# Loads of all 128 rows, paced loads at the start, n1 visits of three halves, and an n2 visit between transform and last stage

## The chip, the cores and the metric

One core of one Trainium2 chip. The metric is the device time of one execution in microseconds, median of several runs; lower is better.

## The reference

```python
# x: (8, 6336, 128), h: (6336, 128)
y = irfft(rfft(x, n=2*S, axis=1) * rfft(h, n=2*S, axis=0), n=2*S)[:, :S]   # causal convolution per channel
scores = y @ w_gate
for b in range(8):
    top = argpartition(-scores[b], 128)[:128]          # 128 rows of each batch
    xe = y[b, top]
    ye = maximum(xe @ w1, 0) @ w2                      # 128 -> 1024 -> 128
    out[b, top] = y[b, top] + sigmoid(scores[b, top])[:, None] * ye
```

## The kernel before

The convolution is done by transforms written as matmuls. 6336 = 99 x 64, so a transform over time is one over n1 (99 points) and one over n2 (64 points). A **unit** is two batches times 64 channels; there are eight (i = 0 to 7). The filter h is treated like one more unit, ahead of them. A unit comes in eight **blocks** of eight channels, each a load of 120 rows of 4 KB (`load_x`, g counts blocks: 0 to 7 are h, 8 to 15 unit 0, and so on). A row holds two halves, `fold` makes their difference (L154, into another buffer) and their sum (L156, in place), on VectorE or GpSimd.

Stages of a unit:

- **n1 transform**, `stage_a`: a block is two **halves** (q = 0, 1); a half is 16 matmuls (L167) into one of three PSUM buffers `pb` and a copy to SBUF by ScalarE (L176), or VectorE (L173).
- **n2 transform**, `stage_b`: 13 chunks of up to 8 of the 99 frequencies. A chunk is 32 matmuls (L204), four products with h's transform on VectorE (L213, which free the PSUM buffer) and two sums on GpSimd (L224). It then loads the table and the h piece three chunks ahead (`load_w` L190, `load_h` L196).
- **inverse n2**, `stage_c`: 16 **items** of 16 matmuls (L308), each ended by ScalarE's copy (L312). Between them, `weigh` sums the scores on VectorE (64 instructions a unit, L292).
- **inverse n1** or last stage, `stage_d`: 16 items (L338), every two of them copied (L349) and stored.

A traced matmul of 32-bit data is two passes, so a half shows as 32 matmuls on the profile's timeline, and an item as 32.

The eight units run as a software pipeline. In the loop of unit i there are 32 items: 0 to 15 are `stage_c` of unit i, 16 to 31 its `stage_d`. Into them a hand-written plan puts **visits** of unit i+1: n1 visits of one block (two halves) ahead of items 0, 1, 3, 4, 6, 7, 9 and 10, and n2 visits of two chunks ahead of items 12, 14, 17, 19, 22, 24 and 27 (the last of one chunk). Items 1 to 6 also issue the first tables and h pieces of unit i+1. Each engine and SP's DMA queue run their instructions in the order written. `load_x(g + 5)` follows a block's n1 visit and waits for it, since there are five load buffers (`RX`).

Scores, the choice of 128 rows (`pick`, a search by counting in eleven steps, each some VectorE work and one small matmul, L414), the gathers, the expert's matmuls (L530, L542) and the scatters run as coroutines. `aside()` lets them issue their next step when an estimate of TensorE's time (`t["pe"]`) has passed the time they gave. Units 2, 4 and 6 carry the end of a search in their first half, units 3, 5 and 7 two experts.

Ahead of the loop, 16 blocks (h and unit 0) are loaded, folded on VectorE and transformed, with five warm-up matmuls before them; then `stage_b_first` (L254) does n2 for h and unit 0 together. All 16 loads are issued at once, as far as SP's queue takes them:

```python
sp.dma_start(out=fa, in_=fa_d)
for g in range(16):
    load_x(g)
```

## Time and profile before

| | us |
|---|---|
| runs (median of 3) | 947.28 |
| runs, lowest and highest | 943.19, 947.48 |
| the profiled execution | 941.33 |
| its span, first to last instruction | 939.5 |

The page gives, for one execution, each engine's busy time, TensorE's granted clock (PEclk, in tenths of full speed), the DMA queues, and groups of instructions by source line. The other views answer for a stretch of time: busy time by stretch, waits with what ended them ("issue" means that the profile shows nothing that the engine waited for), the timeline, and the chain of work that ended last. In `out<-in` the names are the program's tiles: `xr` a loaded block, `slots` the large buffer of transforms, `two` fold results, `pb` a PSUM buffer, `tx` products, `ht` h pieces, `at` and `tab_wb` tables.

### The profile page before, as it was taken

Reading aid. Unit: us, or ns where it says so; the run is one execution under the profiler, and the core shown is the slowest. Engines: PE = TensorE matmul, PEld = TensorE weight load, DVE = VectorE, ACT = ScalarE, POOL = GpSimd, SP = SyncE. Lnnn points to the kernel's source line nnn. Section 1 sums busy time; section 2 is a strip of 40 time slices with the busy share of each in tenths; the row PEclk is TensorE's granted clock in tenths of the full one; section 3 lists DMA queues with packets and bytes.
Section 4 is the critical chain, followed back from the end, with each engine's and each line's share of the span. In section 5 each row is a group of like instructions: output and inputs, shape, how many; then the busy total and the mean of one; then the engine's idle time right before and its main releaser. Section 6 shows DMA issues by size and latency. Waiting matters only on the chain.

```text
span 939.5 us, 37070 instructions
## 1 busy us (share of the span) xinstructions
PE 882.4 (94%) x16558; PEld 777.0 (83%) x16558; DVE 674.3 (72%) x1571; ACT 348.5 (37%) x405; POOL 344.3 (37%) x292
## 2 busy tenths in 40 slices
PE   7789899999998989999999899998999999999996
PEld 5689898889886878878987798887987798879875
DVE  5558966757596996756479897756559898687571
ACT  3533562147211741145411462135511373115321
POOL 0048426612463026620546027640346204460103
PEclk8699999999999999999999999999999999999999
DMA  8759767767574846765566665747457464751051
GB/s 215 195 182 331 219 173 227 246 167 203 169 247 162 235 116 195 240 184 145 139 191 203 177 171 178 260 151 182 109 155 262 147 175 121 238 171 52 16 178 42
DMA packets 66513, 168.38 MB, mean 179 GB/s; under 512 B 9713, under 2 KB 26063, under 8 KB 66354
## 3 DMA queue, kind: packets, MB, share of 16 engines
q1 hardware_dynamic: 65330, 164.96, 59.2%
q8 instruction: 130, 2.13, 1.0%
q0 software_dynamic: 1024, 1.05, 0.4%
q14 instruction: 29, 0.24, 0.1%
HBM read 133.02 MB, written 32.96 MB: 177 GB/s over the span
## 4 chain that ended last, share of the span: by engine, by line
PE 74%; DVE 16%; issue 5%; ACT 2%; DMA 2%; POOL 1%; POOLq 0%; ACTq 0%; DVEq 0%
PE pb L338 21%; PE pb L308 21%; PE pb L204 14%; PE pb L167 10%; DVE acc L292 5%; PE pb L254 4%; DVE tx L213 2%; DVE slots L213 2%; DVE cmp L405 2%; PE m L530 1%; ACT slots L312 1%; PE m L542 1%; DVE xr L156 1%; DMA slots<-tab_wb 1%; DVE num L408 1%
## 5 line engine op out<-in xcount | busy, mean ns | idle before, releaser
L224 POOL TENSOR_TENSOR slots<-slots,tx 128x512 f32<-128x512 f32 (+1 forms) x182 | 231.5, 1304 | 213.6 <-DVE tx L213 200.0
L308 PE MATMUL pb<-wc,slots 64*99 64x128 f32 x4096 | 254.0, 276 | 6.9 <-DVE tx L213 5.1
L308 PEld LDWEIGHTS pb<-wc,slots 64*99 64x99 f32 x4096 | 232.5, 169 | 19.5 <-issue 4.7
L338 PE MATMUL pb<-slots,at 99*99 99x256 f32 (+1 forms) x1040 | 234.3, 376 | 11.1 <-ACT slots L312 9.8
L338 PEld LDWEIGHTS pb<-slots,at 99*99 99x99 f32 x1040 | 159.7, 163 | 63.1 <-ACT slots L312 11.5
L312 ACT COPY slots<-pb 99x1024 f32<-99x1024 f32 x128 | 143.4, 1121 | 177.2 <-PE pb L308 156.8
L204 PEld LDWEIGHTS pb<-slots 128*64 128x64 f32 x5544 | 169.8, 137 | 19.9 <-issue 16.0
L204 PE MATMUL pb<-slots 128*64 128x64 f32 x5544 | 177.5, 222 | 5.9 <-DVE tx L213 3.4
L292 DVE SCALAR_TENSOR_TENSOR acc<-slots,wgl,acc 128x198 f32<-128x198 f32 x496 | 179.0, 436 | 0.9 <-POOL slots L224 0.9
L213 DVE TENSOR_TENSOR slots<-pb,ht 128x512 f32<-128x512 f32 (+1 forms) x182 | 120.0, 660 | 80.8 <-PE pb L204 59.0
L349 ACT COPY yt<-pb 99x1024 f32<-99x1024 f32 x63 | 63.9, 1015 | 306.6 <-PE pb L338 304.0
L176 ACT COPY slots<-pb 128x792 f32<-128x792 f32 x138 | 117.1, 904 | 40.9 <-PE pb L167 40.9
L213 DVE TENSOR_TENSOR tx<-pb,ht 128x512 f32<-128x512 f32 (+1 forms) x182 | 119.6, 657 | 0.0
L167 PE MATMUL pb<-fa,xr 50*64 50x99 f32 x1952 | 102.7, 255 | 9.0 <-issue 8.1
L167 PEld LDWEIGHTS pb<-fa,xr 50*64 50x64 f32 x1952 | 90.8, 138 | 17.7 <-issue 12.1
L154 POOL TENSOR_TENSOR two<-xr 120x512 f32<-120x512 f32 x12 | 25.5, 2129 | 143.1 <-PE pb L167 143.1
L167 PE MATMUL pb<-fa,two 50*64 50x99 f32 x1344 | 69.6, 253 | 0.0
L167 PE MATMUL pb<-fa,slots 50*64 50x99 f32 x1312 | 55.1, 278 | 13.4 <-issue 13.4
L546 POOL DMA_INDIRECT out<-xe,iu x16 | 16.2, 1012 | 132.5 <-DVE xe L544 129.5
L269 POOL TENSOR_TENSOR slots<-slots,tx 128x256 f32<-128x256 f32 (+1 forms) x50 | 39.4, 810 | 65.0 <-DVE tx L266 63.8
L167 PEld LDWEIGHTS pb<-fa,slots 50*64 50x64 f32 x1312 | 50.1, 156 | 15.9 <-issue 14.6
L167 PEld LDWEIGHTS pb<-fa,two 50*64 50x64 f32 x1344 | 61.0, 136 | 0.2 <-issue 0.2
(140 smaller groups left out, 613.7 us busy)
## 6 DMA issues: line engine op xcount, KB each, us to landing
slots<-tab_wb SPq DMA_DIRECT2D x86, 512.0 KB
xr<-in_x SPq DMA_DIRECT2D x61, 480.0 KB
out<-yt SPq DMA_DIRECT2D x63, 396.0 KB
ht<-hd SPq DMA_DIRECT2D x84, 256.0 KB
at<-tab_at SPq DMA_DIRECT2D x128, 153.1 KB
hd<-slots SPq DMA_DIRECT2D x12, 512.0 KB
xr<-tab_wb SPq DMA_DIRECT2D x9, 512.0 KB
slots<-in_h SPq DMA_DIRECT2D x8, 480.0 KB
```

Source lines behind the costliest of these rows:

```text
L167: pe.matmul(pt[c * 64:c * 64 + 64, b, d * N1:(d + 1) * N1], src, fa[rows, c], start=True, stop=True)
L176: act.copy(out=dst, in_=src)
L204: pe.matmul(banks[c][g * 64:g * 64 + 64, j * 64:j * 64 + 64], wt[:, j, c * 64:c * 64 + 64], y[:, g, :, k0 + j], start=True, stop=True)
L213: v.tensor_tensor(out=dst, in0=banks[c][:, 0:kn * 64].rearrange("p (k b j t) -> p k b j t", k=kn, b=2, t=2), in1=ht[t].rearrange("p k (j t ...
L224: pool.tensor_tensor(out=d3, in0=d3, in1=tx.rearrange("p k (j t) -> p k j t", t=2), op=ALU.add if c else ALU.subtract)
L254: pe.matmul(pair[g * 64:g * 64 + 64, c, j * 128:j * 128 + 128], wt[:, q + j, c * 64:c * 64 + 64], both[:, :, g, :, k0 + q + j], start=True ...
L269: pool.tensor_tensor(out=d3, in0=d3, in1=tx[:, c, 0:w].rearrange("p k (j t) -> p k j t", t=2), op=ALU.add if c else ALU.subtract)
L292: v.scalar_tensor_tensor(out=dst, in0=col, scalar=w, in1=dst, op0=ALU.mult, op1=ALU.add)
L308: pe.matmul(pair[0:N1, g, s % 4 * 128:s % 4 * 128 + 128], y[rows, s // 2, ri, :, s % 2], wc[rows, ri], start=(ri == 0), stop=(ri == 1))
L312: act.copy(out=z[:, s // 4], in_=pair[0:N1].rearrange("p g (j t m) -> p (g j) t m", j=2, t=2))
L338: pe.matmul(pt[0:N1, o:o + w * 128], ats[tau // 2][:, tau % 2, c], z[:, c, q:q + w], start=(c == 0), stop=(c == 1))
L349: act.copy(out=yt.rearrange("p n b q d -> p n q b d"), in_=src.rearrange("p (n q b d) -> p n q b d", n=w, q=4, b=2))
```

## The change

- A block's load and folds take all 128 rows instead of 120 (rows 114 to 127 hold zeros in DRAM already).
- At the start four loads are issued; each later one comes behind a fold. A memset of one element of its buffer on VectorE, right behind that fold, is what the load waits for. The memset `ones16` moves behind six folds; the warm-up is 48 matmuls of 64 columns instead of 5 of 512, on a smaller memset.
- n1 visits are of three halves ahead of items 0, 2, 4 and 6 and of four ahead of item 8. Folds and loads go along with their blocks.
- n2 visits at 14, 17, 19, 22, 24 become 14, 16, 19, 22, 25: the one at 16 stands between the last item of `stage_c` and the first of `stage_d`.
- The first tables and h pieces of the next unit are issued at items 1, 3, 5, 7, 9 and 10, not 1 to 6.
- In the last unit `aside()` is called in every step of the last stage, and twice ahead of item 16; the second expert of unit 7 is held before its output matmuls until item 16.

```diff
-    def load_x(g):
+    def load_x(g, paced=False):
...
-        sp.dma_start(out=raw[g][0:XR], in_=src[0:XR, n].rearrange("p (s d n) -> p s d n", s=2, d=8))
+        if paced:
+            v.memset(raw[g][0:1, 0, 0, 0:1], 0.0)
+        sp.dma_start(out=raw[g], in_=src[:, n].rearrange("p (s d n) -> p s d n", s=2, d=8))
...
-    def stage_a(g, r, dve=()):
-        a, o = raw.pop(g), odd.pop(g)
+    def stage_a(g, r, dve=(), halves=(0, 1)):
+        a, o = raw[g], odd[g]
         n = g % 8
-        for q in range(2):
+        for q in halves:
...
-                if w == 2 and tau != 2:
+                if (w == 2 and tau != 2) or i == NU - 1:
                     aside()
...
-                for _ in g:
+                for n, _ in enumerate(g):
                     yield after_act(1.7)
+                    while work is apart and g is todo[1] and n == 2 and place[0] < 16:
+                        yield 1
...
-        for g in range(16):
+        for g in range(4):
             load_x(g)
-        plain = acc.rearrange("p t b c k -> p (t b c k)")
+        plain = acc.rearrange("p t b c k -> p (t b c k)")[:, 0:128]
         v.memset(plain, 1.0)
-        for _ in range(5):
-            pe.matmul(psb()[:, 0], plain[:, 0:128], plain[:, 0:512], start=True, stop=True)
-        v.memset(ones16, 1.0)
+        for _ in range(3):
+            pt = psb()
+            for k in range(16):
+                pe.matmul(pt[:, k // 8, k % 8 * 64:k % 8 * 64 + 64], plain, plain[:, 0:64], start=True, stop=True)
         for g in range(6):
             fold(g, v)
+            load_x(g + 4, True)
+        v.memset(ones16, 1.0)
         for g in range(16):
             if g < 10:
                 fold(g + 6, v)
+                if g < 6:
+                    load_x(g + 10, True)
...
-                for n, at_item in enumerate((0, 1, 3, 4, 6, 7, 9, 10)):
-                    plan[at_item] = [("a", n)]
+                for n, at_item in enumerate((0, 0, 0, 2, 2, 2, 4, 4, 4, 6, 6, 6, 8, 8, 8, 8)):
+                    plan.setdefault(at_item, []).append(("a", n))
...
+                if i == NU - 1 and item == 16:
+                    ready[1] = 0.0
+                    aside()
+                    aside()
...
-                            g = g0 + k
-                            if g % 8 < 6:
+                            g, q = g0 + k // 2, k % 2
+                            if q == 0 and g % 8 < 6:
                                 fold(g + 2, v)
                                 on_dve(1.4)
-                            elif g % 8 == 7:
+                            elif q == 0 and g % 8 == 7:
                                 fold(g + 1, pool)
-                            stage_a(g, (i + 1) % 2)
-                            load_x(g + RX)
-                            if g % 8 == 7:
+                            stage_a(g, (i + 1) % 2, (), (q,))
+                            if q:
+                                load_x(g + RX)
+                            if q and g % 8 == 7:
                                 fold(g + 2, pool)
```

What moves, on the engines' own queues (line numbers of the changed kernel are one or more higher).

VectorE at the very start, before:

```order
L603 MEMSET acc 128x792
L606 MEMSET ones_84 128x128
L154 TENSOR_TENSOR slots<-slots 120x512
L156 TENSOR_TENSOR slots<-slots 120x512
L154 TENSOR_TENSOR slots<-slots 120x512
```

and in the changed kernel, where L139 is the memset that a load waits for:

```order
L606 MEMSET acc 128x128
L155 TENSOR_TENSOR slots<-slots 128x512
L157 TENSOR_TENSOR slots<-slots 128x512
L139 MEMSET slots 1x1
L155 TENSOR_TENSOR slots<-slots 128x512
L157 TENSOR_TENSOR slots<-slots 128x512
L139 MEMSET slots 1x1
```

The first memset is shorter, the second has gone behind the sixth fold, and each fold pair is followed by one tiny memset.

TensorE at the turn from `stage_c` (L308) to `stage_d` (L338) in the loop of unit 0, with the n2 visits (L204) of unit 1, before:

```order
L308 MATMUL pb<-wc,slots 99x128 x32
L204 MATMUL pb<-slots 64x64 x64
L308 MATMUL pb<-wc,slots 99x128 x32
L338 MATMUL pb<-slots,at 99x128 x4
L338 MATMUL pb<-slots,at 99x256 x2
L204 MATMUL pb<-slots 64x64 x64
L338 MATMUL pb<-slots,at 99x256 x8
```

and in the changed kernel (L309, L339 and L205 are the same lines):

```order
L309 MATMUL pb<-wc,slots 99x128 x32
L205 MATMUL pb<-slots 64x64 x64
L309 MATMUL pb<-wc,slots 99x128 x32
L205 MATMUL pb<-slots 64x64 x64
L339 MATMUL pb<-slots,at 99x128 x4
L339 MATMUL pb<-slots,at 99x256 x10
```

The visit has moved from behind the first item of the last stage to ahead of it.

ScalarE in the first half of unit 0, where L176 copies a half and L312 an item, before:

```order
L176 COPY slots<-pb 128x2x2x2x99 x2
L312 COPY slots<-pb 99x4x2x128
L176 COPY slots<-pb 128x2x2x2x99 x2
L312 COPY slots<-pb 99x4x2x128 x2
L176 COPY slots<-pb 128x2x2x2x99 x2
```

and in the changed kernel (L177 and L313):

```order
L177 COPY slots<-pb 128x2x2x2x99 x3
L313 COPY slots<-pb 99x4x2x128 x2
L177 COPY slots<-pb 128x2x2x2x99 x3
L313 COPY slots<-pb 99x4x2x128 x2
L177 COPY slots<-pb 128x2x2x2x99 x3
```

Two halves to one or two items have become three halves to two items.

## Rows read from the trace of the kernel before

**Rows 1.** The page: section 1 (busy time of each engine) and the instruction queue of section 3.

```profile
PE 882.4 (94%) x16558; PEld 777.0 (83%) x16558; DVE 674.3 (72%) x1571; ACT 348.5 (37%) x405; POOL 344.3 (37%) x292
...
q8 instruction: 130, 2.13, 1.0%
```

**Rows 2.** Busy time by stretch: stretch, length, busy (count) by engine, PEclk, DMA share, GB/s.

```profile
0.00:53.20 53.20, 38.80 (x1034) 33.08 (x1034) 27.95 (x39) 23.52 (x27) 0.20 (x4) 0.81 0.77 201
...
308.00:364.00 56.00, 50.87 (x1220) 47.93 (x1218) 51.29 (x122) 29.56 (x32) 15.38 (x12) 0.97 0.67 184
...
85.00:90.00 5.00, 5.00 (x92) 5.00 (x90) 4.14 (x13) 1.51 (x3) 3.90 (x6) 1.00 1.00 351
```

**Rows 3.** TensorE's waits in units 0 to 6: total us, times, longest.

```profile
PE pb L167 <- issue: 8.9, 5, 3.6
PE pb L338 <- ACT slots L312: 8.3, 7, 1.2
...
PE pb L338 <- DVE tx L213: 1.3, 3, 0.4
```

**Rows 4.** Timeline of TensorE in the start: start us, us, instructions, idle before.

```profile
18.49 5.55 PE L167 MATMUL pb<-fa,slots 50*64 50x99 f32 x127 [4.12 <-issue]
26.80 5.01 PE L167 MATMUL pb<-fa,slots 50*64 50x99 f32 x127 [2.76 <-issue]
34.83 2.09 PE L167 MATMUL pb<-fa,slots 50*64 50x99 f32 x44 [3.02 <-issue]
...
47.19 3.04 PE L167 MATMUL pb<-fa,slots 50*64 50x99 f32 x127 [0.80 <-issue]
51.90 1.41 PE L167 MATMUL pb<-fa,slots 50*64 50x99 f32 x51 [1.67 <-issue]
...
54.47 5.75 PE L254 MATMUL pb<-slots,xr 128*64 128x128 f32 x96 [0.80 <-DVE slots L173]
```

**Rows 5.** DMA queues from 5 to 35 us: packets, MB, share of 16 engines.

```profile
DMA packets 1918, 7.04 MB, mean 235 GB/s; under 512 B 208, under 2 KB 208, under 8 KB 1915
...
q1 hardware_dynamic: 1915, 6.99, 95.7%
q8 instruction: 3, 0.05, 0.8%
```

**Rows 6.** Timeline of VectorE in the start, the folds of blocks.

```profile
5.77 0.69 DVE L154 TENSOR_TENSOR slots<-slots 120x512 f32<-120x512 f32 x1 [3.93 <-DMA slots<-in_h]
6.50 0.69 DVE L156 TENSOR_TENSOR slots<-slots 120x512 f32<-120x512 f32 x1
7.91 0.69 DVE L154 TENSOR_TENSOR slots<-slots 120x512 f32<-120x512 f32 x1 [0.72 <-DMA slots<-in_h]
...
39.77 0.69 DVE L154 TENSOR_TENSOR slots<-slots 120x512 f32<-120x512 f32 x1 [1.22 <-PE pb L167]
```

**Rows 7.** Groups of instructions: count | busy us, mean ns | idle before.

```profile
L213 DVE TENSOR_TENSOR tx<-pb,ht 128x512 f32<-128x512 f32 (+1 forms) x182 | 119.6, 657 | 0.0
L176 ACT COPY slots<-pb 128x792 f32<-128x792 f32 x138 | 117.1, 904 | 40.9 <-PE pb L167 40.9
```

**Rows 8.** Timeline of TensorE in the units, at four waits.

```profile
154.25 1.99 PE L338 MATMUL pb<-slots,at 99*99 99x128 f32 x12 [1.18 <-ACT slots L312]
...
287.57 2.72 PE L204 MATMUL pb<-slots 128*64 128x64 f32 x46 [3.39 <-DVE tx L213]
...
351.99 3.63 PE L308 MATMUL pb<-wc,slots 64*99 64x128 f32 x32 [3.80 <-DVE tx L213]
...
888.24 2.00 PE L338 MATMUL pb<-slots,at 99*99 99x128 f32 x12 [1.54 <-ACT slots L312]
```

**Rows 9.** The chain that ended last: an n2 visit, an item, an n1 visit.

```profile
383.42 3.93 PE pb L204 x128
...
411.88 1.93 PE pb L308 x32
413.81 1.52 PE pb L167 x62
```

More of the change, by code (lines that the diff above doesn't have):

```diff
@@ L26 @@
 NT = 33
-XR = 120
 ZS = 128 * 128
@@ L143, in fold @@
             return
-        a = raw[g][0:XR]
+        a = raw[g]
         if g < 16:
@@ L151, in fold @@
         odd[g] = o.rearrange("p (d n) -> p d n", d=8)
-        o = odd[g][0:XR]
+        o = odd[g]
         if part < 2:
@@ L629, in conv_moe @@
             if i < NU - 1:
-                for n, at_item in enumerate((0, 1, 3, 4, 6, 7, 9, 10)):
-                    plan[at_item] = [("a", n)]
-                for n, at_item in enumerate((12, 14, 17, 19, 22, 24, 27)):
+                for n, at_item in enumerate((0, 0, 0, 2, 2, 2, 4, 4, 4, 6, 6, 6, 8, 8, 8, 8)):
+                    plan.setdefault(at_item, []).append(("a", n))
+                for n, at_item in enumerate((12, 14, 16, 19, 22, 25, 27)):
                     plan[at_item] = [("b", k) for k in range(2 * n, min(NC, 2 * n + 2))]
@@ L644, in conv_moe @@
                     load_constants(2)
-                if i < NU - 1 and 1 <= item < 7:
-                    (load_h if item % 2 == 0 else load_w)((i + 1) % 2, (item - 1) // 2)
+                if i < NU - 1 and item in (1, 3, 5, 7, 9, 10):
+                    k = (1, 3, 5, 7, 9, 10).index(item)
+                    (load_h if k % 2 else load_w)((i + 1) % 2, k // 2)
                 if 0 <= item - at_first < RA:
                     load_at(item - at_first)
+                if i == NU - 1 and item == 16:
+                    ready[1] = 0.0
+                    aside()
+                    aside()
                 if item in plan:
```

## The prediction

> **What bounds the kernel now.** I read the page first, then the busy times by stage, then the waits of TensorE, and last the timelines at the places that these named. TensorE is busy for 882.4 us, 94% of the span [rows 1], so the kernel is TensorE's queue with holes in it, and the question is which holes the change closes. The profiled execution took 941.33 us, 1.8 us more than its span; the three other runs took 943.19 to 947.48 us. The sum below is made on 941.33 and moved by +4 us at the end, about the middle between the profiled run and the median.
>
> The holes lie in three places. First the start: in the first 53.2 us TensorE is busy for 38.8 us at a mean clock of 0.81 [rows 2]. Second the eight units: between 104 and 845 us TensorE waits 8.9 us for nothing that the profile shows, always in front of the n1 transform, 8.3 us for ScalarE in front of the last stage, and 1.3 us there for product buffers [rows 3]. Third, units 2, 4 and 6 have a first half in which VectorE itself is nearly full: 51.29 of 56 us [rows 2].
>
> In the start, three pauses of 4.12, 2.76 and 3.02 us stand in front of runs of about 127 matmuls, with no releaser [rows 4]. The page counts 130 packets on the instruction queue, and matmuls and weight loads together 33,116: one packet for every 255 instructions, or 127 matmuls with their weight loads [rows 1]. So I read these pauses as TensorE waiting for its next packet of instructions while the loads fill the DMA engines: from 5 to 35 us only 3 such packets moved, with the engines 95.7% taken by the loads [rows 5]. The runs of 127 start 8.0 to 8.3 us apart there. At 47 to 52 us, where 512 KB loads run, they start 4.71 us apart [rows 4].
>
> **The change, part by part.**
>
> Loads of 128 rows. A block of 120 rows arrives every 2.13 us (the folds of h start at 5.77, 7.91 and so on, each waiting for its load) [rows 6], and the stretch with only such loads moves 235 GB/s [rows 5]. The kernel's 128-row traffic between 85 and 90 us, mostly 512 KB pieces, moves 351 GB/s [rows 2]. A block of 524,288 bytes would take 1.49 us at that rate, 2.23 us at the old one. I take 1.5 us, because the traffic at 85 to 90 us goes in the same 128 pieces of 4 KB as the new loads. The Trainium skill (DMA: Bandwidth & Descriptors, "Why a DMA increments its semaphore by 16 and not by 1") says that a transfer is spread over the largest count up to 16 that divides its outer dimension: 15 for 120 rows, 16 for 128. By that alone each engine moves eight rows either way, a block still takes 2.13 us and the start gives nothing, as in rival (2); the two rates in the rows differ by far more than 16 to 15, which only a run can explain.
>
> Four loads ahead. VectorE gets one tiny memset behind each of the first twelve folds, and each load from the fifth waits for its own memset. The trace has none so small; between 0 and 0.2 us each, I take 0.1 us. A fold pair holds VectorE for 1.4 us [rows 6], so it needs 1.5 us a block, as the loads do. The first block lands some 0.6 us sooner (2.13 less 1.5), so folding begins near 5.1 us, the sixteenth fold near 5.1 + 15 x 1.55 = 28.4 us and ends near 29.8 us; before, it began at 39.77 us [rows 6]. Behind the waiting loads on SP stand only the next loads and the first table loads, which wait for TensorE anyway. What is late next is ScalarE: the first ten blocks give it 20 copies of 904 ns [rows 7], about 18.4 us, from some 9.7 us on, to 28 us. Then six blocks at TensorE's 1.52 us [rows 9] and a copy on VectorE end near 38.5 us. That is the best case. The worst is 8.0 us a packet until the loads end: by 28.4 us only some seven blocks are through (two and a half from the packets that are there at the start, then two per 8 us from 18.5 us on), and the other nine, at 1.52 us and shorter pauses, end near 46 us. I take 42.5 us, by the 4.71 us spacing beside fast loads. The second stage begins at 54.47 us now [rows 4]: **-12 us**, ends -8 and -16. The warm-up of 48 narrow matmuls instead of 5 wide ones, the shorter memset ahead of it and the memset moved behind six folds have only VectorE's and TensorE's wait for the first load to fill, so 0.
>
> The visit between the stages. In units 0 to 6 the last stage begins with a wait of 1.18 us for ScalarE's last copy (154.25 is one of seven) [rows 8]. The change puts the n2 visit of 64 matmuls, 3.93 us long [rows 9], into that place, so the copy is covered. The visit needs a buffer that the one two items before has used; VectorE frees it 1.96 + 2 x 4 x 0.66 = 7.2 us after that visit began [rows 7], and TensorE comes back after 3.93 + 2 x 1.93 = 7.8 us [rows 9]. So it just fits. The visit's table and h loads are issued by the visits at items 12 and 14, at least 7 us ahead. 7 x 1.18 = 8.3; I take **-7 us** (0 to -8.3). In the last unit the second expert's 8 output matmuls go into the same gap, 1.54 us [rows 8]: **-1.5**.
>
> Three halves to a visit. TensorE's work is the same: two items and three halves are 2 x 1.93 + 3 x 0.76 = 6.1 us [rows 9]. A half's copy is 904 ns [rows 7], so three halves in a row leave ScalarE some 0.5 us behind, four 0.6 us, and the items behind them give that back before the three buffers come round. Eight blocks are through at item 8 instead of 10. The folds come earlier, so VectorE has no less to do before the first n2 visit: in unit 2 it frees that visit's buffers at 351.99 us after 45 us without a pause, and TensorE waits 3.80 us [rows 8]. That hole does not close: VectorE has the same work in front of it. Part of it moves to the visit at item 8, whose last fold now has 33 weighings ahead of it on VectorE instead of 38, while TensorE gets there 3.8 us sooner. **0** (0 to +3).
>
> Loads spread out. Until item 4 a unit now issues 4 x blocks, one table and one h load, where it issued 4, 2 and 2: 2.8 MB instead of 3.5, and the x part at 1.5 us instead of 2.13 us a block. The pauses without releaser in the units, five of 8.9 us in all and 3.6 us at most [rows 3], all stand in front of the n1 transform, where these loads run, and after a pause TensorE runs slower for a while: 32 passes took 3.63 us after the wait of 3.80 us [rows 8] against 1.93 elsewhere [rows 9], as at half the granted clock. Against it, item 8 issues 64 transform matmuls without an item between: 128 passes and as many weight loads in 3.04 us, where 4.2 us was the shortest for a packet. I take **-4 us** (+4 to -8.9).
>
> Small ones. The n2 visits of the last stage stand three items apart; that covers the 1.3 us for product buffers [rows 3] and gives the 3.39 us wait of unit 1 one item, 1.8 us, more room [rows 8]: **-3** (0 to -4.7).
>
> Sum: 12 + 7 + 1.5 + 4 + 3 = 27.5; 941.33 - 27.5 = 913.8 us as profiled, **918 us** for a median. All good ends together: 16 + 8.3 + 1.5 + 8.9 + 4.7 = 39.4, 906 us. All bad ends together: 8 + 1.5 - 4 - 3 = 2.5, 943 us.
>
> **Rivals.**
>
> (1) The refill stays slow: loads land faster, but a packet of instructions keeps taking 8 us while they run. For it: three packets in 30 us. Against: 4.71 us beside faster loads. The start gives 8 instead of 12 and the units nothing for their pauses: -19.5, **926 us**.
>
> (2) The 120 rows are not what makes those loads slow, since both x and h are read with 32 KB from row to row. Then a block takes 2.23 us, the last fold begins near 5.9 + 15 x 2.23 = 39.4 us as before, and the start gives nothing: -15.5, **930 us**. Against: no row of the trace separates pitch from row count. The Trainium skill has a rule here that speaks against the change (DMA: Bandwidth & Descriptors, "Latency and other measured facts": large power-of-two row pitches slow DMA copies; its figures begin at 512 KiB); no run here shows it yet.
>
> (3) The change does not cover the turn: a search step of VectorE slips between the products of the visits at items 14 and 16 and takes more than the 0.6 us to spare, so that a wait for VectorE of about the old size replaces the 1.18 us for ScalarE. The order shows the steps at items 12 and 16, so the price is the seven turns, +7 us: **925 us**.
>
> (4) Slower: the visit of four halves at item 8 outruns the instruction packets in every unit. A pause like the longest, 3.6 us [rows 3], with the slow passes after it costs 3.6 + 1.7 = 5.3 us; one in each of seven units is 37 us against the 27.5 gained, and it decides from 4 us per unit on: **955 us**. Against: five such waits in all seven units now, and the shortened interval is at one place in a unit.
>
> **How the numbers follow.** Forecast 0.63, (1) 0.18, (2) 0.08, (3) 0.07, (4) 0.04. The range 903 to 935 us holds the forecast with its good ends and the first three rivals; it leaves out (4) and the all-bad corner. A measurement of this kernel can tell about 0.5%, here below 942.5 or above 952.0 us. Only (4) and the corner are not faster: faster 0.93, same 0.04, slower 0.03.
>
> **What would show it.** Folds of the start 1.5 to 1.6 us apart and the second stage beginning at 39 to 46 us; no TensorE wait for ScalarE's copy at the turns; fewer than 5 us without releaser in the units; the wait of VectorE in units 2, 4 and 6 still there, some of it in front of the n1 transform. The prediction is wrong if folds stay 2.1 us apart, if the turn has a wait for VectorE, or if pauses in front of the n1 transform grow past 20 us.

## The result, and the profile after

| | us |
|---|---|
| before, median of 4 runs beside it | 945.24 |
| after, median of 4 runs (lowest, highest) | 918.71 (917.17, 921.89) |
| after / before, with 95% interval | 0.973 (0.968 to 0.979) |
| the profiled execution of after, its span | 921.89, 920.1 |

The forecast was 918 us. By the ratio the change gave 25 us (20 to 31) where the sum had 27.5. The two profiled executions, on which the readings below rest, differ by 19.4 us; that of after was the longest of its four, that of before shorter than three of the four runs beside it. The terms of the sum did not hold: in these profiles the start, which was to give 12 us, cost 4.5 us, and the units gave 24 us where 15.5 had been counted for them.

In the kernel after, lines stand one higher up to the loop (L168 is L167 of before, L309 is L308, L339 is L338, L214 is L213); the warm-up is L610. First the busy time by stretch (stretch, length, busy time and count by engine, PEclk, DMA share, GB/s), of before: the start, units 0, 1, 3 and 4.

```profile
0.00:100.08 100.08, 84.89 (x1826) 78.73 (x1827) 63.68 (x135) 37.73 (x51) 35.18 (x49) 0.90 0.77 231
100.08:200.26 100.18, 96.03 (x1949) 84.36 (x1948) 66.09 (x148) 38.39 (x41) 44.41 (x36) 1.00 0.69 205
200.26:306.27 106.01, 100.73 (x1975) 88.52 (x1974) 80.31 (x177) 38.89 (x40) 39.12 (x30) 0.98 0.68 197
...
410.29:526.08 115.79, 111.04 (x2041) 96.56 (x2040) 82.69 (x187) 42.04 (x52) 43.15 (x34) 0.99 0.59 172
526.08:629.43 103.35, 98.75 (x1964) 86.77 (x1964) 80.47 (x184) 38.75 (x40) 48.21 (x34) 0.98 0.66 192
```

The same stretches of after:

```profile
0.00:104.59 104.59, 96.82 (x1912) 94.62 (x1912) 62.51 (x147) 36.98 (x51) 35.17 (x49) 0.97 0.66 228
104.59:201.75 97.16, 95.15 (x1949) 84.29 (x1948) 66.30 (x148) 38.60 (x41) 47.20 (x36) 1.00 0.67 214
201.75:300.97 99.22, 97.39 (x1975) 86.43 (x1974) 81.11 (x177) 38.82 (x40) 42.92 (x30) 1.00 0.68 213
...
404.59:514.47 109.88, 108.58 (x2041) 95.25 (x2040) 83.89 (x187) 42.14 (x52) 43.88 (x34) 1.00 0.58 184
514.47:617.21 102.74, 97.29 (x1965) 86.62 (x1964) 82.87 (x183) 38.56 (x40) 42.36 (x34) 0.97 0.62 196
```

Read the lengths first: the start grew by 4.5 us; unit 0 lost 3.0 us, unit 1 6.8 us, unit 3 5.9 us, unit 4 only 0.6 us. Then TensorE's busy time for the same passes: in unit 3 it fell by 2.5 us, in unit 1 by 3.3 us. So in these two profiles a unit gains in two ways, by shorter waits and by passes that run faster. The PEclk of the start cannot be read so: the view prints 1.00 wherever the trace holds no clock record, and the first record, a rise to 1.00, stands at 7.2 us in before and at 27.9 us in after. Counts of TensorE's passes tell the level ahead of it. Two stretches of after ahead of and behind 27.9 us, then one of before with a recorded 0.50, all in the n1 transform:

```profile
24.00:26.00 2.00, 2.00 (x56) 2.00 (x56) 1.26 (x2) 1.17 (x2) 0.00 (x0) 1.00 0.00 0
28.00:30.00 2.00, 2.00 (x104) 2.00 (x100) 1.63 (x5) 1.89 (x4) 0.00 (x0) 1.00 0.66 223
```

```profile
20.00:22.00 2.00, 2.00 (x56) 2.00 (x52) 1.27 (x2) 1.24 (x2) 0.00 (x0) 0.50 0.94 223
```

The 56 passes in 2 us ahead of 27.9 us are as many as at 0.50 in before. So TensorE of after ran at the lower of its two levels (1.2 GHz) until 27.9 us, through the whole warm-up and 6 us of the n1 transform.

What happened in the start stands in the timelines of after, first TensorE's (start us, us, instructions, idle before it), then VectorE's with the folds.

```profile
1.06 20.74 PE L610 MATMUL pb<-acc 128*128 128x64 f32 x96 [1.06 <-DVE acc L606]
21.74 11.74 PE L168 MATMUL pb<-fa,slots 50*64 50x99 f32 x380
...
56.45 13.79 PE L255 MATMUL pb<-slots,xr 128*64 128x128 f32 x192 [0.55 <-DVE slots L174]
```

```profile
4.87 0.69 DVE L155 TENSOR_TENSOR slots<-slots 128x512 f32<-128x512 f32 x1 [3.86 <-DMA slots<-in_h]
...
6.23 0.69 DVE L155 TENSOR_TENSOR slots<-slots 128x512 f32<-128x512 f32 x1
...
7.57 0.69 DVE L155 TENSOR_TENSOR slots<-slots 128x512 f32<-128x512 f32 x1
...
24.71 0.69 DVE L155 TENSOR_TENSOR slots<-slots 128x512 f32<-128x512 f32 x1 [9.47 <-PE pb L168]
```

Blocks are folded every 1.34 us instead of 2.13 [rows 6], so the loads did become faster. But the 96 passes of the new warm-up, 216 ns apart, hold TensorE until 21.7 us. VectorE folds what it has buffers for, then waits 9.5 us for TensorE to use the first of them. The second stage begins at 56.45 us, against 54.47 [rows 4].

In units 0 to 6 the list of TensorE's waits (total us, times, longest) shrank; its four largest lines of nine:

```profile
PE pb L309 <- DVE tx L214: 11.3, 3, 5.5
PE pb L168 <- issue: 1.6, 5, 0.4
PE pb L339 <- DMA at<-tab_at: 1.2, 1, 1.2
PE pb L205 <- issue: 1.2, 4, 0.4
```

Against [rows 3]: the seven waits for ScalarE at the turn (8.3 us) are gone, those for product buffers (1.3 us) too, and the pauses without releaser in front of the n1 transform fell from 8.9 to 1.6 us. One wait grew in this profile: behind the first n2 visit of units 2 and 4 an item waits for VectorE to free that visit's buffers, 3.80 us in unit 2 before [rows 8], now 5.48 and 5.45 us. Behind it the granted clock stands at 0.50, as this row on the stretch behind the longer one shows:

```profile
346.50:348.50 2.00, 1.95 (x18) 1.98 (x20) 2.00 (x4) 0.00 (x0) 2.00 (x3) 0.50 0.41 128
```

### The profile page after: what moved, and what is told of

Read it like the earlier page. It is cut to its first block, busy times and chain, and to the rows that moved or that the text cites. A ratio compares the mean times of both kernels' runs of the same rounds, so it can differ in the third digit from the quotient of the medians.

```text
span 920.1 us, 37274 instructions
## 1 busy us (share of the span) xinstructions
PE 884.2 (96%) x16644; PEld 789.7 (86%) x16644; DVE 683.6 (74%) x1583; ACT 347.9 (38%) x405; POOL 345.5 (38%) x292
## 4 chain that ended last, share of the span: by engine, by line
PE 79%; DVE 13%; issue 3%; DMA 2%; POOL 1%; ACT 0%; SPq 0%; POOLq 0%; ACTq 0%; DVEq 0%
PE pb L339 24%; PE pb L309 19%; PE pb L205 17%; PE pb L168 9%; DVE acc L293 7%; PE pb L255 4%; PE pb L610 2%; PE m L533 1%; PE m L545 1%; DMA slots<-tab_wb 1%; DVE cmp L406 1%; DVE two L155 1%; DVE xr L157 1%; PE m L364 1%; DVE num L409 1%
## 5 line engine op out<-in xcount | busy, mean ns | idle before, releaser
L309 PE MATMUL pb<-wc,slots 64*99 64x128 f32 x4096 | 247.5, 275 | 13.0 <-DVE tx L214 11.3
L309 PEld LDWEIGHTS pb<-wc,slots 64*99 64x99 f32 x4096 | 230.5, 169 | 22.7 <-issue 12.6
L339 PE MATMUL pb<-slots,at 99*99 99x256 f32 (+1 forms) x1040 | 232.6, 376 | 1.2 <-DMA at<-tab_at 1.2
L313 ACT COPY slots<-pb 99x1024 f32<-99x1024 f32 x128 | 143.5, 1121 | 169.3 <-PE pb L309 156.5
L339 PEld LDWEIGHTS pb<-slots,at 99*99 99x99 f32 x1040 | 160.3, 163 | 52.7 <-DMA at<-tab_at 1.7
L293 DVE SCALAR_TENSOR_TENSOR acc<-slots,wgl,acc 128x198 f32<-128x198 f32 x496 | 186.1, 450 | 2.6 <-POOL slots L225 2.6
L205 PEld LDWEIGHTS pb<-slots 128*64 128x64 f32 x5544 | 169.1, 136 | 15.3 <-issue 13.0
L214 DVE TENSOR_TENSOR slots<-pb,ht 128x512 f32<-128x512 f32 (+1 forms) x182 | 119.7, 658 | 79.9 <-PE pb L205 68.3
L205 PE MATMUL pb<-slots 128*64 128x64 f32 x5544 | 176.5, 222 | 2.1 <-issue 1.2
L177 ACT COPY slots<-pb 128x792 f32<-128x792 f32 x138 | 114.2, 918 | 34.1 <-PE pb L168 31.0
L214 DVE TENSOR_TENSOR tx<-pb,ht 128x512 f32<-128x512 f32 (+1 forms) x182 | 119.0, 654 | 0.0
L168 PE MATMUL pb<-fa,xr 50*64 50x99 f32 x1952 | 94.5, 248 | 3.1 <-issue 2.2
L168 PEld LDWEIGHTS pb<-fa,xr 50*64 50x64 f32 x1952 | 85.7, 133 | 9.8 <-issue 6.7
L155 POOL TENSOR_TENSOR two<-xr 128x512 f32<-128x512 f32 x12 | 27.4, 2287 | 119.8 <-PE pb L168 96.3
L168 PE MATMUL pb<-fa,two 50*64 50x99 f32 x1344 | 67.3, 248 | 0.7 <-issue 0.7
L270 POOL TENSOR_TENSOR slots<-slots,tx 128x256 f32<-128x256 f32 (+1 forms) x50 | 39.4, 809 | 69.5 <-DVE tx L267 68.3
L168 PEld LDWEIGHTS pb<-fa,two 50*64 50x64 f32 x1344 | 59.0, 132 | 1.1 <-issue 1.1
L168 PE MATMUL pb<-fa,slots 50*64 50x99 f32 x1312 | 49.2, 260 | 4.9 <-issue 4.9
L168 PEld LDWEIGHTS pb<-fa,slots 50*64 50x64 f32 x1312 | 45.5, 143 | 6.2 <-issue 5.8
```

The lines of the kernel that those rows point to most:

```text
L168: pe.matmul(pt[c * 64:c * 64 + 64, b, d * N1:(d + 1) * N1], src, fa[rows, c], start=True, stop=True)
L177: act.copy(out=dst, in_=src)
L205: pe.matmul(banks[c][g * 64:g * 64 + 64, j * 64:j * 64 + 64], wt[:, j, c * 64:c * 64 + 64], y[:, g, :, k0 + j], start=True, stop=True)
L214: v.tensor_tensor(out=dst, in0=banks[c][:, 0:kn * 64].rearrange("p (k b j t) -> p k b j t", k=kn, b=2, t=2), in1=ht[t].rearrange("p k (j t ...
L270: pool.tensor_tensor(out=d3, in0=d3, in1=tx[:, c, 0:w].rearrange("p k (j t) -> p k j t", t=2), op=ALU.add if c else ALU.subtract)
L293: v.scalar_tensor_tensor(out=dst, in0=col, scalar=w, in1=dst, op0=ALU.mult, op1=ALU.add)
```

## The experiments

All ratios are against runs of the kernel before beside them, with 95% intervals. "Rest" is the span less the start of unit 0 in the one profiled execution. It scatters: after, wide_warm, wide_warm_at_once, short_warm, no_warm and narrow_w64 have the same code behind the start, and their rest lies between 803.7 and 818.9 us. One profile doesn't tell differences of the rest below some 15 us apart; there the ratios decide. The start scatters too: in the five kernels with the old start (before, loop_only, turn_only, halves_only, spread_only) unit 0 begins between 99.54 and 103.28 us. "Stage two begins" is the start of its first long run of passes.

| kernel | ratio | stage two begins | unit 0 begins | rest |
|---|---|---|---|---|
| before | 1 | 54.47 | 100.08 | 839.4 |
| after | 0.973 (0.968 to 0.979) | 56.45 | 104.59 | 815.5 |
| wide_warm | 0.961 (0.957 to 0.965) | 46.75 | 92.35 | 803.7 |
| wide_warm_at_once | 0.961 (0.956 to 0.965) | 46.52 | 91.97 | 807.2 |
| short_warm | 0.961 (0.956 to 0.967) | 45.22 | 90.67 | 818.9 |
| no_warm | 0.963 (0.957 to 0.968) | 45.40 | 90.85 | 813.0 |
| narrow_w64 | one run | 46.17 | 93.30 | 814.4 |
| start_only | 0.997 (0.995 to 0.9995) | 58.82 | 104.28 | 829.6 |
| rows_128 | 0.987 (0.983 to 0.991) | 44.93 | 90.48 | 838.3 |
| split_rows | 0.992 (0.989 to 0.996) | 50.63 | 96.17 | 835.8 |
| loop_only | 0.972 (0.966 to 0.978) | 54.52 | 103.09 | 812.9 |
| turn_only | 0.994 (0.990 to 0.999) | 53.99 | 99.54 | 829.9 |
| halves_only | 0.992 (0.987 to 0.996) | 54.09 | 100.91 | 830.3 |
| spread_only | 0.995 (0.990 to 1.001) | 55.02 | 103.28 | 840.0 |

### What the warm-up costs

**wide_warm**: the kernel after with the old warm-up and the old, longer memset ahead of it.

```
-        plain = acc.rearrange("p t b c k -> p (t b c k)")[:, 0:128]
+        plain = acc.rearrange("p t b c k -> p (t b c k)")
-        for _ in range(3):
-            pt = psb()
-            for k in range(16):
-                pe.matmul(pt[:, k // 8, k % 8 * 64:k % 8 * 64 + 64], plain, plain[:, 0:64], start=True, stop=True)
+        for _ in range(5):
+            pe.matmul(psb()[:, 0], plain[:, 0:128], plain[:, 0:512], start=True, stop=True)
```

> The changed kernel with the old warm-up (5 matmuls of 512 columns) and nothing else put back. Theory: the 48 narrow matmuls hold TensorE until 21.7 us and are all that keeps the start from gaining; without them the n1 transform starts near 9 us, the second stage near 42 us instead of 56.45, and the kernel takes about 905 us (902 to 909). Rival: the start is bound by TensorE's instruction packets whatever the warm-up; then it gains 5 us at most, 914 us or more.

Measured: 902.38 us, ratio 0.961; the intervals of wide_warm and after do not touch. The theory holds, but stage two begins at 46.75 us and not near 42. The runs of the kernel before beside it took 937.69 us, so against the 945.24 us of the result 0.961 is some 908 us. Its timeline of TensorE:

```profile
1.75 7.36 PE L608 MATMUL pb<-acc 128*128 128x512 f32 x10 [1.75 <-DVE acc L606]
9.04 5.06 PE L168 MATMUL pb<-fa,slots 50*64 50x99 f32 x211
...
46.75 17.46 PE L255 MATMUL pb<-slots,xr 128*64 128x128 f32 x300 [0.80 <-DVE slots L174]
```

Ten passes of 512 columns end 12.7 us sooner than 96 of 64, and stage two begins 9.7 us sooner. The new warm-up cost what the faster loads brought, and this kernel beats both.

**start_only**: the kernel before with the new start (128 rows, paced loads, new warm-up) and the old plan of the units.

```
-XR = 120
...
-        for g in range(16):
+        for g in range(4):
             load_x(g)
...
-            pe.matmul(psb()[:, 0], plain[:, 0:128], plain[:, 0:512], start=True, stop=True)
+                pe.matmul(pt[:, k // 8, k % 8 * 64:k % 8 * 64 + 64], plain, plain[:, 0:64], start=True, stop=True)
...
+            load_x(g + 4, True)
...
+                if g < 6:
+                    load_x(g + 10, True)
```

> The kernel before with the loads of 128 rows (in the whole program), the paced start and the new warm-up alone. Theory: the start loses 2 to 5 us by the warm-up and the units gain at most what their pauses cost: 940 to 949 us, no clear change. Rival: 128-row loads take the units' pauses away, 933 to 938 us.

Measured: ratio 0.997, a gain of 2.6 us (0.5 to 4.8); unit 0 begins at 104.28 us as in after. The start of the change as a whole is worth next to nothing. The theory holds by the ratio; 935.76 us lies in the rival's range only because the runs of before beside it took 937.69 us. The rival is right about the pauses: in the units none without releaser is left, but waits of 9.9 us for VectorE and 5.5 us for a table stand in that profile.

**short_warm** keeps one of three rounds of the narrow warm-up, **no_warm** none (the loop taken out).

```
-        for _ in range(3):
+        for _ in range(1):
             pt = psb()
             for k in range(16):
```

> The changed kernel with one of its three rounds of warm-up left, 16 small products (32 passes) instead of 48. Theory (the warm-up costs by its length: 96 passes 216 ns apart hold TensorE until 21.7 us while four blocks wait folded): 32 passes end at about 8.0 us, before VectorE has folded its third block, stage two begins at 43 to 47 us instead of 56.5, and the total is 9 to 15 us under that of the changed kernel, about that of the wide warm-up (ratio to the kernel before 0.955 to 0.967). Rival (the narrow form is the fault and not the length, by what it leaves TensorE's clock or queue in): stage two begins after 52 us and the ratio stays above 0.968.

> The changed kernel with no warm-up at all. Theory (a warm-up that ends before the first folds are done costs nothing, and so its absence gains nothing but what TensorE's clock makes of it): within 5 us of the kernel with one round of warm-up, stage two between 42 and 50 us. Rival A: without it TensorE runs the first transforms at half speed long enough that stage two begins 6 us or more later than with one round. Rival B: the warm-up is useless and the start is 3 us or more shorter.

TensorE's first rows of short_warm, then of no_warm:

```profile
1.06 7.09 PE L610 MATMUL pb<-acc 128*128 128x64 f32 x32 [1.06 <-DVE acc L606]
8.09 7.05 PE L168 MATMUL pb<-fa,slots 50*64 50x99 f32 x190
```

```profile
6.66 10.15 PE L168 MATMUL pb<-fa,slots 50*64 50x99 f32 x348 [6.66 <-DVE slots L139]
```

Stage two at 45.22 and 45.40 us, ratios 0.961 and 0.963. The form does no harm if it is short, and without any warm-up the start is as good: what decides is whether the warm-up ends before the blocks wait. Rival A of no_warm is right that the first transforms run at half speed, but only until its first clock record at 10.7 us, as the pass counts on either side show, and stage two begins only 0.2 us later than in short_warm; rival B falls.

```profile
8.70:10.70 2.00, 2.00 (x60) 2.00 (x56) 1.97 (x6) 1.41 (x2) 0.00 (x0) 1.00 0.92 295
10.80:12.80 2.00, 2.00 (x104) 2.00 (x100) 1.35 (x4) 1.84 (x3) 0.00 (x0) 1.00 1.01 365
```

**narrow_w64**: the kernel after, the 48 warm-up products with weights of 64 columns instead of 128.

```
-                pe.matmul(pt[:, k // 8, k % 8 * 64:k % 8 * 64 + 64], plain, plain[:, 0:64], start=True, stop=True)
+                pe.matmul(pt[0:64, k // 8, k % 8 * 64:k % 8 * 64 + 64], plain[:, 0:64], plain[:, 0:64], start=True, stop=True)
```

> The changed kernel with the weights of its 48 warm-up products halved from 128 columns to 64, the moved data the same 64 columns. If the load of the weights sets the 216 ns between passes, they come about 110 ns apart, the warm-up ends at about 12 us and stage two begins 7 to 10 us sooner than in the changed kernel. Rival (the moved columns, or a fixed price of a pass, set it): 216 ns as before, end at 21.7 us, and a total within 4 us of that of the changed kernel.

Its row on TensorE's timeline, and under it the group row (count, busy us, mean ns) of the warm-up's weight loads in after:

```profile
1.06 7.80 PE L610 MATMUL pb<-acc 128*64 128x64 f32 x96 [1.06 <-DVE acc L606]
```

```profile
L610 PEld LDWEIGHTS pb<-acc 128*128 128x128 f32 x96 | 20.6, 333 | 1.1 <-DVE acc L606 1.1
```

96 passes take 7.80 us instead of 20.74, 81 ns apart instead of 216, and stage two begins 10.3 us sooner than in after. The 81 ns are a mean over two clock levels: the first clock record of narrow_w64 stands at 5.5 us, in the middle of its warm-up. Rows ahead of and behind it:

```profile
1.10:5.40 4.30, 4.30 (x41) 4.30 (x42) 0.23 (x1) 0.92 (x1) 0.00 (x0) 1.00 0.82 249
5.50:8.70 3.20, 3.20 (x57) 3.20 (x56) 3.10 (x8) 0.00 (x0) 0.00 (x0) 1.00 1.03 399
```

That is some 105 ns a pass at the lower level and 56 ns at the higher. In after the level stays low through the whole warm-up, so the like comparison is 216 against 105 ns: with the same 64 moved columns, half the width of the weights halves the price, as the expectation had it (about 110 ns). The Trainium skill (TensorE: Matmul & The Clock Gate, "LDWEIGHTS (loading the stationary operand)") has the load's time go by its columns; an estimate from its formula is 107 ns for 128 columns and 53 ns for 64. The proportion agrees; the spacings here are about twice the estimate, and no row splits a pass into its load and its products. It is no price of the shape alone: n2 passes with weights of 64 columns and 64 moved columns, written in turn to the two halves of the partitions of their buffer, come 31 ns apart at the higher level (128 in 3.93 us) [rows 9].

### What the loads are worth

**rows_128**: the kernel before with one number changed.

```
-XR = 120
+XR = 128
```

> The kernel before with one number changed: every load and fold of the rows takes 128 rows instead of 120; all sixteen loads still go out at once, the old warm-up stands, the units' plan is untouched. Theory (the 120-row transfer is what makes the loads slow, and its slow tail inside the units is what stretches TensorE's issue pauses at the n1 visits): a block arrives every 1.3 to 1.5 us instead of 2.1, stage two begins at 45 to 48 us instead of 54.5, the pauses of 2.1, 2.4 and 3.7 us in the units shrink under 1 us each, and the total falls by 14 to 22 us against the kernel before of the same session (ratio 0.977 to 0.985). Rival (128 rows help the start alone): 7 to 10 us, ratio 0.989 to 0.993, with the pauses in the units as before.

Measured: ratio 0.987, 12.6 us. Stage two begins at 44.93 us, 9.5 us sooner. Rows on a stretch that holds only such loads, before and then here:

```profile
20.00:30.00 10.00, 7.24 (x177) 6.94 (x173) 6.16 (x9) 4.78 (x6) 0.00 (x0) 0.50 0.97 234
```

```profile
10.00:20.00 10.00, 7.11 (x231) 6.76 (x227) 8.99 (x14) 6.05 (x9) 0.00 (x0) 0.79 1.03 410
```

The pitch from row to row is 32 KB in both. So 128 rows instead of 120 raise the rate by three quarters, and the rival (2) of the prediction falls. In the units the pauses in front of the n1 transform shrink as the theory had it, but waits for a table come up (0.5 us in before, 5.1 here), those for VectorE stay at about the same sum, and the rest stays (838.3 us), as the rival had it. The ratio lies between the two. TensorE's largest waits of rows_128 in units 0 to 6:

```profile
PE pb L338 <- ACT slots L312: 8.3, 7, 1.2
PE pb L308 <- DVE tx L213: 7.9, 2, 4.7
PE pb L204 <- DMA slots<-tab_wb: 5.1, 3, 4.4
PE pb L167 <- issue: 1.9, 2, 1.2
```

**split_rows**: the kernel before, each load of 120 rows as one of 112 and one of 8.

```
+        for lo, hi in ((0, 112), (112, XR)):
+            sp.dma_start(out=raw[g][lo:hi], in_=src[lo:hi, n].rearrange("p (s d n) -> p s d n", s=2, d=8))
```

> The kernel before with each load of 120 rows split into one of 112 rows and one of 8; the folds, the sixteen loads at once, the warm-up and the plan as before. If the count of rows has to divide by 16 for the load to spread over all 16 DMA engines: the 112 rows go at the fast rate and the 8 rows cost little beside them, so blocks arrive 1.3 to 1.6 us apart and stage two begins by 49 us (ratio 0.984 to 0.992). Rival: what the 128-row load gains is not the spread, and the split with twice the transfers arrives at 2.1 us a block or later, stage two at 54 us or after (ratio 0.997 to 1.01).

Its row on the stretch of loads, and its DMA packets from 5 to 30 us:

```profile
20.00:30.00 10.00, 8.72 (x218) 8.22 (x210) 7.21 (x11) 6.23 (x8) 0.00 (x0) 0.59 1.02 265
```

```profile
DMA packets 1914, 6.59 MB, mean 264 GB/s; under 512 B 314, under 2 KB 314, under 8 KB 1911
```

Between the two expectations: 265 GB/s, stage two at 50.63 us, ratio 0.992. Divided by 16 engines and their busy share, an engine moves 15.1 GB/s with 120 rows (234 / 16 / 0.97), 16.2 split, 24.9 with 128 rows. The packets under 512 bytes come to about 15 a block of 120 rows [rows 5] (208 for 14.2 blocks), 24 a block here (314 for 13.3 blocks). That fits the Trainium skill (DMA: Bandwidth & Descriptors, "Why a DMA increments its semaphore by 16 and not by 1"), 15 engines for 120 rows and 16 + 8 for the split; but an estimate from its count makes 128 rows only 16/15 faster, and measured is 1.75; and the 112 rows, 16 engines by that count, did not bring the rate of 128. Why an engine's packets take so much longer with 120 rows stays open.

**wide_warm_at_once**: wide_warm with all sixteen loads issued at once.

```
-        for g in range(4):
+        for g in range(16):
             load_x(g)
...
-            load_x(g + 4, True)
...
-                if g < 6:
-                    load_x(g + 10, True)
```

> As wide_warm, but all 16 first loads issued at once instead of four ahead. Theory: the depth of the load queue is what holds TensorE's instruction packets back; pauses of 2 to 4 us return and the start is 4 to 8 us longer than in wide_warm. Rival: pacing does nothing once the loads are fast: within 2 us of wide_warm.

Ratio 0.9606 against 0.9610, stage two 0.2 us apart: the rival holds. Holding loads back behind the folds gives nothing once they are fast.

### What the plan of the units is worth

**loop_only**: the kernel before with the new plan of the units alone (120 rows, old start).

```
-                for n, at_item in enumerate((0, 1, 3, 4, 6, 7, 9, 10)):
+                for n, at_item in enumerate((0, 0, 0, 2, 2, 2, 4, 4, 4, 6, 6, 6, 8, 8, 8, 8)):
...
-                for n, at_item in enumerate((12, 14, 17, 19, 22, 24, 27)):
+                for n, at_item in enumerate((12, 14, 16, 19, 22, 25, 27)):
...
-                if i < NU - 1 and 1 <= item < 7:
+                if i < NU - 1 and item in (1, 3, 5, 7, 9, 10):
```

> The kernel before with the new plan of the eight units alone (visits of three halves, the n2 visit between the stages, spread table loads, the last unit's changes); loads of 120 rows, all at once at the start, old warm-up. Theory: the whole gain lies here, about -24 us, 921 us (917 to 926). Rival: the units' pauses went because 128-row loads leave the DMA engines free sooner; then the plan alone keeps the pauses, and takes 930 us or more.

Measured: ratio 0.972, 26 us (21 to 32): the theory holds, and it is all of the change's gain. Of the rival this much is true: with 120 rows the pauses in front of the n1 transform fall only from 8.9 to 5.8 us, and 3.8 us stand in front of items. The product of rows_128 and loop_only is 0.9867 x 0.9719 = 0.959, which is wide_warm_at_once (0.9606): the two parts add up.

**turn_only** (n2 visits at 16 and 25 instead of 17 and 24), **halves_only** (the first pair of lines above) and **spread_only** (the third) take the plan apart.

> The kernel before with two numbers of the plan changed: the n2 visits of items 17 and 24 move to 16 and 25. Theory: the six waits of TensorE for ScalarE of 1.2 us at the turn go, and since the wait for VectorE in units two and four grows by what the turn gave, the total falls by 4 to 7 us, ratio 0.992 to 0.996. Rival A: the visit at the turn carries most of what the units gained, 12 us or more, ratio under 0.988. Rival B: nothing is left of it, ratio 0.997 to 1.003.

> The kernel before with the n1 visits alone changed: three halves of a block at items 0, 2, 4 and 6, four at item 8, instead of a whole block at eight items; the units' other loads, the n2 visits and the start are as before. Theory from the prediction (the visits were priced at nothing, 0 to +3 us): ratio 0.998 to 1.004. Rival: the visits are where the units gained more than forecast, since five visits make fewer places at which TensorE's queue runs dry than eight; then 6 to 14 us, ratio 0.985 to 0.994, and the pauses of 2.1 to 3.7 us at the first n1 visits shrink.

> The kernel before with the loads of tables for the next unit alone moved: from items 1 to 6, one each, to items 1, 3, 5, 7, 9 and 10. Theory from the prediction (4 us, between 8.9 lower and 4 higher): ratio 0.991 to 1.0, the pauses of 2.1, 2.4 and 3.7 us in the units shrink below 2 us each. Rival: the loads of the rows themselves, not those of the tables, set the pauses; then the pauses stay and the ratio is 0.998 to 1.002.

turn_only: 0.994, 5.3 us (1.3 to 9.2), the size that the theory had. In its units no TensorE wait for ScalarE is left, nor one for product buffers, and unit 1's 3.39 us [rows 8] are gone. What took back the rest was not what was expected: in its profile the wait for VectorE in front of items fell, from 5.1 to 2.6 us, and the pauses without releaser grew, from 9.6 to 14.5 us.

halves_only: 0.992, 7.9 us (3.5 to 12.5). The rival holds in its size, but only partly by its reason. The sums of units 0 to 5 (length, busy times), of before and of halves_only:

```profile
sum 646.14, PE 616.06 PEld 540.05 DVE 474.08 ACT 238.71 POOL 260.18; mean PE 51.34 PEld 45.00 DVE 39.51 ACT 19.89 POOL 21.68
```

```profile
sum 634.15, PE 608.26 PEld 535.60 DVE 478.93 ACT 239.18 POOL 274.26; mean PE 50.69 PEld 44.63 DVE 39.91 ACT 19.93 POOL 22.85
```

The units are 12.0 us shorter. Of that 4.2 us are waits: those for VectorE shrank, those without releaser grew from 9.6 to 11.6 us. The other 7.8 us are TensorE's busy time for the same passes. This split is from one profile of each: the six kernels with the same units spread over 10.7 us in the length of units 0 to 5 and over 5.5 us in their busy time, so it points at the passes and does not settle their share. Rows around the first pause of unit 3 show how a pause makes passes slower; before, then halves_only:

```profile
420.30:422.30 2.00, 0.31 (x13) 0.31 (x16) 1.90 (x6) 0.64 (x1) 0.00 (x0) 1.00 0.96 242
422.30:424.30 2.00, 2.00 (x50) 1.88 (x42) 1.31 (x3) 0.91 (x1) 0.00 (x0) 0.84 0.54 146
424.30:426.30 2.00, 2.00 (x28) 1.73 (x28) 1.97 (x8) 0.37 (x1) 0.00 (x0) 0.50 0.90 226
426.30:428.30 2.00, 2.00 (x66) 1.87 (x60) 2.00 (x7) 1.67 (x3) 0.00 (x0) 0.81 0.53 132
```

```profile
412.40:414.40 2.00, 1.21 (x22) 0.94 (x17) 1.97 (x6) 1.39 (x2) 0.00 (x0) 1.00 0.88 243
414.40:416.40 2.00, 2.00 (x40) 2.00 (x38) 2.00 (x7) 0.97 (x2) 0.00 (x0) 1.00 0.86 183
416.40:418.40 2.00, 2.00 (x70) 1.86 (x70) 1.38 (x3) 1.34 (x2) 0.00 (x0) 1.00 1.03 249
```

Behind a pause of 2.14 us the granted clock fell to 0.50 and stayed there for 3.4 us; here the same place has a pause of 0.79 us and the clock stays at 1.00. The length of a pause alone does not say it: in halves_only a pause of 2.24 us in unit 2 left the clock at 1.00, one of 2.31 us in unit 4 took it to 0.50. What else decides it is open.

spread_only: 0.995, from 9.6 us lower to 0.6 higher, so neither theory nor rival is decided by the time. Its pauses in front of the n1 transform shrink to 4.8 us, but 6.9 us of waits for a table come up, and the rest is 840.0 us. The three ratios multiply to 0.981, loop_only has 0.972: the parts may help each other (a wait that one part moves is taken up by another), or it lies in the intervals; that was not settled.

## Why the prediction was right in sum and wrong in its terms

- **The start, -12 us (ends -8 and -16).** The mechanism was right, its size at the low end: with the old warm-up stage two begins 9.5 us (rows_128) or 7.7 us (wide_warm) sooner. The block takes 1.34 us where 1.5 was counted. Pauses between instruction packets remain, 1.06, 1.06 and 2.78 us in wide_warm while the loads run, but the runs of 127 passes start 4.2 and 5.8 us apart, and not the 8 us a packet of rival (1). The clock of 0.81 that the prediction read for the start counts the 7.2 us ahead of the first record as full speed. The 20 copies of ScalarE are 18.1 us, not 18.4, which changes nothing.
- **The warm-up, 0: this step failed.** It was taken to fill a wait for the first load and got no duration. It lasts 20.7 us, and the first block is folded at 6.3 us. Nor did it warm anything up: the clock was still low when it ended, where the old warm-up brought it up at 7.4 us (wide_warm). Unit 0 begins at 104.59 us with it and at 92.35 with the old one: 12.2 us, more than the start's gain. The trace of before had the row to bound it, and the prediction did not use it: the old warm-up's weight loads, as wide as the new one's, had this group row.

```profile
L605 PEld LDWEIGHTS pb<-acc 128*128 128x128 f32 x10 | 2.9, 298 | 5.3 <-issue 3.6 <-DVE acc L603 1.8
```

  96 passes with a weight load each, at 298 ns, would have been an estimate of 28.6 us. The prediction put the term at nothing without pricing the passes or their weight loads.
- **The turn, -7, and the small ones, -3.** turn_only carries both: 5.3 us (1.3 to 9.2) by the runs where 10 were counted. The mechanism was right, all the waits they named are gone; the size was about half, since in that profile pauses without releaser grew by 4.9 us.
- **The last unit, -1.5.** Unit 7 takes 95.45 us against 94.55 (loop_only: 93.95). The wait for ScalarE at 888.24 us [rows 8] went, but in no profile is the unit more than 0.7 us shorter than in before; not run alone.
- **Three halves to a visit, 0 (0 to +3): the mis-sized term.** It gave 7.9 us. The bounds reached only upward, since waits alone were weighed. By the rows of halves_only a visit's place also bears on how long a pause is, and with that on how long TensorE runs at half clock; the prediction had that for the loads, and not for the visits. How much of the 7.9 us it makes stays open.
- **Loads spread out, -4 (+4 to -8.9).** The pauses shrank as said, from 8.9 to 1.6 us in after. By itself neither half of it shows in the rest: with 128 rows alone it is 1.1 us shorter, with spread tables 0.6 us longer, both less than one profile tells, and waits for a table of 5.1 and 6.9 us come up.
- **The hole in units 2, 4 and 6 does not close**: right for units 2 and 4. In unit 2 it grew from 3.80 to 5.48 us, which fits that units 2 and 4 gained only 0.4 and 0.6 us; in wide_warm, with the same units, the longest is 3.8 us.
- **Rivals.** (2) falls with rows_128, (3) with the turn's clean rows. (4) falls too: no pause of over 0.4 us is left in front of the n1 transform in the units. (The 4.2 us a packet that the prediction set against (4) stands in no row shown; 4.71 us is the shortest there.)

So two errors of opposite sign met: the warm-up, counted at 0, took 12 us, and the units gave more than the 15.5 us counted, 24 us in the profiles and 26 us by loop_only. That the sum came out at 918 us is luck. With the warm-up mended, the change gives 37 us (33 to 41) by the ratio of wide_warm, near the all-good end of the sum (39.4 us).

## What to carry to other kernels

Price an operation of a shape that the trace does not have by the part of it that the trace does have, here the weight load, and multiply by the count before writing "hidden". A warm-up is free only up to the moment the first real input is ready; here none was needed at all. Weigh a pause of TensorE by the clock behind it as well as by its length. And check a clock of 1.00 by the count of passes: where a trace has no clock record yet, the view prints 1.00 all the same.

## What the runs showed of the hardware

- Loads of 120 rows of 4 KB move 234 GB/s, of 128 rows 410 GB/s, at the same pitch of 32 KB. Splitting off 112 rows brings 265.
- 32-bit passes of the warm-up with 64 moved columns come 216 ns apart with weights of 128 columns (96 in 20.74 us) and some 105 ns apart with weights of 64 (41 in 4.30 us), both at the lower clock level; the latter come 56 ns apart at the higher (57 in 3.20 us).
- 96 passes with weights of 128 columns over 20.7 us left TensorE at the lower level; it rose 6 us into the n1 transform behind them (after). With the ten passes of 512 columns it rose at 7.4 us, while they ran (wide_warm).
- Without any warm-up the first n1 passes begin at 6.66 us, as soon as the first block is folded, and run at the lower level until 10.7 us: 60 passes in 2 us, then 104 (no_warm).
